# Scatters declared independent, and the gathers of the conditional pairs put into their first product

## The chip, the cores and the metric

The kernel runs on one core of one Trainium2 chip. Its time is the device time of one execution in microseconds (us); less is better. Three runs of the kernel before took 545.45, 544.35 and 548.22 us, a median of 545.45 us.

## What is computed

An attention block reads 32 states per head into 512 tokens and the tokens into the states, with two softmaxes. The rows that it makes, 8 x 544 = 4352 of 512 numbers, go to a mixture of 8 experts. Each row belongs to one expert, which depends on the row itself and, through a gate, on the row before it:

```python
for b in range(B):
    prev_e = -1
    for s in range(S):
        fresh_e = int(np.argmax(logits[b, s]))
        if s == 0 or local_gate[b, s] < 0.5:
            e = fresh_e
        else:
            e = prev_e if prev_e >= 0 else fresh_e
        prev_e = e
        ...
        h = np.maximum(x[b, s] @ w1[e], 0.0)
        out[b, s] = p[e] * (h @ w2[e])
```

`w1[e]` is 512 x 1024 and `w2[e]` is 1024 x 512; everything is in 32-bit floats. `p[e]` is the softmax probability of the expert.

## The kernel before, in words

**Stages.** `Attention` makes the rows and writes them to `rows` in device memory. `Routing` finds each row's expert and gives it a slot: rows of one expert are put together in pairs of 128-row blocks, and what is left over goes in tiles of 32 rows. `slots.tok` holds the number of the row in each slot (for whole rows), `slots.row` the same for quarters of rows. `experts` (from line 770) then works through the pairs and tiles. A row has one slot; a slot without a row has a number beyond the table, which the scatter leaves out.

**Pairs.** A pair is two blocks, b = 0 and 1, of rows of one expert. At least 10 pairs (`NPMIN`) and at most 23 (`NP`) can be needed; the number is known only on the chip. `pair` (L1095) is called for pairs 0 to 8 in a plain loop (L1171), each with a 32-row tile between its halves and with `late=True`. Pair 9 and those after it come from `last` (L1174): pair 9 always, and each further one inside a `tc.If(pairs > u + 1)` (L1178), nested; there `late=False`. In this data 16 pairs run, 0 to 15, so the branch to pair 16 is not taken.

**One pair.** Both products of a pair are done with seven half-size products instead of eight. `strassen` (L987) is the first product, `second_half` (L1030) the second, both through `seven` (L946), which runs the products in the order 1, 5, 6, 2, 7, 3, 4 (with `apart`, 1, 5, 6, 2, 3, 7, 4) and lets ScalarE or VectorE (DVE) take each result from PSUM. The sums of quarter matrices that this needs are DVE's: of w1 in `first_sums` (tiles `a`, in two parts), of w2 in `second_sums` (tiles `c`, at the start of a pair), of the turned rows in `column_sums` (tiles `xs`, from `x_t`). All sums come from the helper `add` (L917), so the profile shows them at L918.

**Preparing the next pair.** While pair u computes, SP loads the weights of pair u + 1 (`load`, L851), DVE makes their sums, and POOL gathers the rows: `quarter` (L807) is one indirect DMA of 128 quarter rows into `xgs_`, which has two buffers, for even and odd pairs. `gathers(v, b)` (L818) is a generator of four of these for block b of pair v. Each waits for a value: `tick` (L823) is a one-element copy on POOL of a result of the products, so a gather is issued behind that result. `seven` hands results to `gets` at four places: behind products 5, 6, 2 and 7; with `apart`, behind 5, 6, 2, 3 and 4, of which a generator uses the first four. In pair u, the first product gathers block 1 of pair u + 1, and the second product block 0 of pair u + 2 (L1134, `gets`).

In the second product, `ready(0)` (L1120) makes the first two sums of the next `a`, turns both gathered blocks into `x_t` (`turned`, L837) and makes the `xs` sums; `ready(1)` makes the last two sums of `a`. Both are for pair u + 1, also when that pair does not come.

**Scatters.** A finished block `ys[b]` goes to its rows of `out` by an indirect DMA on POOL: `scatter` (L982), shown at L984. Block 0 is scattered inside the second product, block 1 behind it: with `late=True` it is handed to the next pair, which issues it in its first product (`waiting`), with the tile's scatter (`Tile.scatter`, L912, shown at L914) after it; with `late=False` it is issued at the end of the pair, before the branch. All scatters write `out`. In the order that is kept between operations on one tensor, each waits until the one before it has been written.

**Order.** The order of each engine's work is that of the program (`tc.manual_schedule`, L85). POOL's queue in a conditional pair u is: the scatter of block 1 of the pair before, four ticks and gathers of the first product, a `drain` (L1140), ticks and gathers of the second product, and between them the scatter of block 0. SP's queue holds the weight loads.

Of the kernel before, what the change touches and what calls it, by code (L numbers as in the profile page):

```python
# [23 lines left out]
NT = B * T  # L24
# [9 lines left out]
Q = P // SQ  # L34
PAIR = 2 * P

NPMIN = NT // PAIR - E * (PAIR - 1) // PAIR

NP = (NT + (E - 1) * (PAIR - 1)) // PAIR
# [132 lines left out]
class Attention:  # L172
# [80 lines left out]
    def get(self, name, *key):  # L253
        return self.of[(name, *key)]
# [515 lines left out]
def experts(ctx, late, tc, bank, w1, w2, rows, slots, route, routing, out):  # L770
    nc = tc.nc
# [28 lines left out]
    def places(u, i):  # L800
# [3 lines left out]
        (w11, w12, w21, w22), sums = [[ring[i][(n + j) % RING] for j in js] for js in (range(4), range(4, 7))]  # L804
        return ((w11, w12), (w21, w22)) if i == 0 else ((w11, w21), (w12, w22)), sums

    def quarter(to, k, i):  # L807

        nc.gpsimd.indirect_dma_start(out=to.rearrange("p x k -> p (x k)"), out_offset=None,  # L809
                                     in_=rows.rearrange("n q x -> (n q) x"),  # L810
                                     in_offset=bass.IndirectOffsetOnAxis(ap=slots.row[:, k, i:i + 1], axis=0))
# [6 lines left out]
    def gathers(u, b):  # L818


        for i in range(Q):
            value = yield
            nc.gpsimd.tensor_copy(tick, value)  # L823
            quarter(xgs_[u % 2][:, b, i], 2 * u + b, i)
        while True:
            yield

    def begun(generator):
        next(generator)
        return generator  # L830


    def turned(u):
        for b in range(2):
            to = x_t[:, :, b * P:b * P + P]
            if u:
                nc.vector.transpose(to.rearrange("p k (i t) -> p k i t", i=Q),  # L837
                                    xgs_[u % 2][:, b].rearrange("p i x k -> p k i x"))
                continue

            for h, copy in enumerate((nc.vector.tensor_copy, nc.scalar.copy)):
                t = bank(P, KT * P // 2)
                for j in range(KT // 2):
                    nc.tensor.transpose(t[:, j * P:j * P + P], first[b][:, 2 * h + j::KT], route.ident)
                copy(to[:, 2 * h:2 * h + 2, :], t.rearrange("p (k t) -> p k t", k=KT // 2))
# [5 lines left out]
    def load(u, i, quarters=slice(4)):  # L851

        e = index(slots.experts[0:1, u - 1:u] if u else slots.again if i else slots.expert)
        q = places(u, i)[0]
        for half, other in [((0, 0), (0, 1), (1, 0), (1, 1)), ((0, 0), (1, 0), (0, 1), (1, 1))][i][quarters]:
            to = q[half][other]
            if i:
                w = w2[bass.ds(e, 1), half, :, other]
            else:
                w = w1[bass.ds(e, 1), half, :, other * KT * F // 4:(other + 1) * KT * F // 4]  # L860
            nc.sync.dma_start(out=to.rearrange("p k f -> p (k f)"), in_=w.rearrange("o p x -> (o p) x"))

    class Tile:
# [6 lines left out]
        def gather(self):  # L870
            quarter(self.x_g, self.k, self.q)
# [39 lines left out]

        def scatter(self, y):  # L912
            at = bass.IndirectOffsetOnAxis(ap=slots.row[:, self.k, self.q:self.q + 1], axis=0)
            nc.gpsimd.indirect_dma_start(out=out.rearrange("n (q x) -> (n q) x", q=Q), out_offset=at, in_=y,  # L914
                                         in_offset=None, bounds_check=NT * Q - 1, oob_is_err=False)

    def add(out, a, b, op=Alu.add):  # L917
        nc.vector.tensor_tensor(out, a, b, op=op)  # L918
# [12 lines left out]
    def first_sums(u, part):  # L931
        ((a11, a12), (a21, a22)), to = places(u, 0)
        if part == 0:
            add(to[0], a21, a22)
            add(to[1], to[0], a11, Alu.subtract)
        else:
            add(a21, a11, a21, Alu.subtract)
            add(to[2], a12, to[1], Alu.subtract)

    def column_sums():  # L940
        sums_of_rows(xq, (xs[0], xs[1], xs[3]), lambda b22, b12: add(xs[2], b22, b12, Alu.subtract))

    def second_sums(u):
        sums_of_rows(*places(u, 1), lambda b22, b12: add(b12, b12, b22, Alu.subtract))
# [36 lines left out]

    def scatter(b, y):  # L982
        to = bass.IndirectOffsetOnAxis(ap=slots.tok[:, b:b + 1], axis=0)
        nc.gpsimd.indirect_dma_start(out=out, out_offset=to, in_=y, in_offset=None, bounds_check=NT - 1,  # L984
                                     oob_is_err=False)

    def strassen(u, others, gets, waiting):  # L987
        ((a11, a12), (a21, a22)), was = places(u, 0)
# [41 lines left out]
    def second_half(u, others, ready, gets, behind, late):  # L1030
# [19 lines left out]
        def second_whole(i, t):  # L1050
            if i == 1:
                others(1)
                scaled(ys[0][:, low], p0)(t)
                ready(0)
                if late:
                    ready(1)
                return ys[0]
            elif i == 4:
                add(ys[1][:, high], r7, r5)
            elif i == 2:  # L1060
                nc.vector.scalar_tensor_tensor(ys[0][:, high], t, p0, r2, Alu.mult, Alu.add)
                scatter(2 * u, ys[0])
                return ys[0]
            else:
                if late:
                    scaled(ys[1][:, low], p1)(t)
                else:
                    nc.vector.scalar_tensor_tensor(ys[1][:, low], t, p1, r7, Alu.mult, Alu.add)
                behind.append(lambda: scatter(2 * u + 1, ys[1]))
                return ys[1]  # L1070
# [6 lines left out]
    def plain(u, gets):  # L1077

        a = places(u, 0)[0]
        for b in range(2):  # L1080
            for n in range(2):
                hps = bank()
                for i in range(4):
                    for j in range(KT):
                        nc.tensor.matmul(hps[:, i * P:i * P + P], lhsT=a[n][j // 2][:, j % 2, i * P:i * P + P],
                                         rhs=x_t[:, j, b * P:b * P + P], start=(j == 0), stop=(j == KT - 1))
                nc.scalar.activation(hqs[2 * b + n].rearrange("p m t -> p (m t)"), hps, Act.Relu)
                for get in gets:
                    get(hqs[2 * b + n][:, 0, :])
        add(hs[0], c12, h22)  # L1090
        add(hs[1], hs[0], h11, Alu.subtract)
        add(c12, c12, h11, Alu.subtract)
        add(hs[2], h21, hs[1], Alu.subtract)

    def pair(u, ahead=True, tile=None, after=None, waiting=(), late=True):  # L1095


        behind = []
        if ahead:
            for i in range(2):  # L1100
                load(u + 1, i, slice(2) if u or i else slice(4))
        second_sums(u)
        if tile:
            tile.turned()

        def between():
            if u == 0:
                next(probabilities)
            if tile:
                tile.one()  # L1110
            if after:
                after.load(0)
                after.gather()

        def others(i):

            if ahead:
                load(u + 1, i, slice(2, 4))

        def ready(i):  # L1120
            if ahead:
                first_sums(u + 1, i)
                if i == 0:
                    turned(u + 1)
                    column_sums()

        def getting(v, b):
            if not ahead or v >= NP:
                return lambda value: None
            generator = begun(gathers(v, b))  # L1130
            return lambda value: generator.send(value[0:1, 0:1])


        gets = [getting(u + 1, 1), getting(u + 2, 0)]  # L1134
        if u:
            strassen(u, others, gets[0], waiting)
        else:
            plain(u, [getting(1, 0), gets[0]])
        if not late:
            nc.gpsimd.drain()  # L1140
        between()
        second_half(u, others, ready, gets[1], behind, late)
        if u == 0:
            next(probabilities)
        if tile:
            behind.append(tile.two())
        if after:
            after.load(1)
        if not late:
            for results in behind:  # L1150
                results()
        return behind
# [18 lines left out]
    for u in range(NPMIN - 1):  # L1171
        waiting = pair(u, True, tiles[u], tiles[u + 1] if u + 1 < NTILE else None, waiting)

    def last(u, waiting=()):  # L1174

        pair(u, u + 1 < NP, waiting=waiting, late=False)
        if u + 1 < NP:
            with tc.If(pairs > u + 1):  # L1178
                last(u + 1)
# [35 lines left out]
```

## Time and profile before

| | |
|---|---|
| median of three runs | 545.45 us (544.35 to 548.22) |
| the profiled execution | 547.97 us, of which its span (first to last instruction) 546.2 us |
| granted TensorE clock, mean | 0.996 |
| busy: PE, PEld, DVE, ACT, POOL | 525.4, 459.2, 382.4, 173.7, 318.4 us |
| gathers of quarter rows for pairs (`xg`, L809) | 132, 1197 ns each in the mean |
| scatters of blocks (L984) | 32, 1097 ns each in the mean |
| scatters of tiles (L914) | 9 |

The engines are PE (TensorE's products), PEld (its weight loads), DVE (VectorE), ACT (ScalarE), POOL (GpSimd) and SP (SyncE, which issues the weight loads). In the timeline a line gives the start in us, the duration, the engine, the line of the program, the operation, what it writes and reads, how many, and in brackets the idle time of that engine before it and what ended it. The busy time of a DMA on POOL is the time for which POOL works at issuing it; the landing comes later. In the busy time by stretch, the columns are the stretch, its length, the busy time of PE, PEld, DVE, ACT and POOL (with the number of instructions), the clock, the busy share of the DMA engines and GB/s. A releaser in brackets is inferred; where the engine named had long been done, it was something else, often a DMA.

### The profile page before, as it was taken

The page shows a single profiled execution, that of the slowest core. Times are in us where ns is not written, and L with a number is a line of the kernel's source. Part 1 is how long each engine was busy: PE and PEld are TensorE (multiplying, and loading weights), DVE is VectorE, ACT ScalarE, POOL GpSimd, SP SyncE. Part 2 cuts the span into 40 slices and gives each one's busy share as a digit, 9 for nine tenths or more (in the row PEclk, how much of TensorE's full clock was granted, in tenths as well). Part 3 has the DMA queues.
Part 4 walks back from the last instruction along what each step waited for, and adds up shares of the span by engine and source line. Part 5 has one row for each costly group of instructions (what it writes and reads, how often), then busy time and mean ns, then how long its engine had stood idle before and what let it go on. Part 6 is the DMA issues. An engine that isn't in the chain of part 4 may idle for free. (4 is left out here: it accounts for less than half of the span.)

```text
span 546.2 us, 12964 instructions
## 1 busy us (share of the span) xinstructions
PE 525.4 (96%) x4921; PEld 459.2 (84%) x4921; DVE 382.4 (70%) x622; ACT 173.7 (32%) x357; POOL 318.4 (58%) x386
## 2 busy tenths in 40 slices
PE   7789889999999999999999999999999999999993
PEld 2567666988989898989898989889999998999992
DVE  6999876757666657575665848486767767787773
ACT  6788654112223222222222222313232222223220
POOL 7788602564684756565665656576564645545454
PEclk9999999999999999999999999999999999999998
DMA  8999777699989899897979797974748484666743
GB/s 315 411 341 350 260 254 237 235 395 393 403 285 377 309 340 361 293 387 267 388 276 389 269 385 281 354 235 166 232 168 283 146 286 153 243 201 223 233 158 104
DMA packets 49002, 155.46 MB, mean 285 GB/s; under 512 B 6865, under 2 KB 8017, under 8 KB 45602
## 3 DMA queue, kind: packets, MB, share of 16 engines
q1 hardware_dynamic: 41234, 135.78, 68.0%
q0 software_dynamic: 7552, 18.69, 9.7%
q8 instruction: 41, 0.67, 0.5%
q14 instruction: 31, 0.25, 0.1%
q10 hardware_dynamic: 144, 0.07, 0.1%
HBM read 136.68 MB, written 17.89 MB: 283 GB/s over the span
## 5 line engine op out<-in xcount | busy, mean ns | idle before, releaser
L809 POOL DMA_INDIRECT xg<-rows,row x132 | 158.0, 1197 | 26.5 <-issue 25.6
L918 DVE TENSOR_TENSOR a<-a,a 128x1024 f32<-128x1024 f32 x64 | 77.1, 1225 | 29.7 <-DMA a<-in_w_dram 28.3
L1001 PE MATMUL ps<-xt,a 128*128 128x128 f32 x720 | 88.8, 276 | 0.0
L1001 PE MATMUL sum<-xs,a 128*128 128x128 f32 x720 | 87.7, 275 | 0.0
L1001 PEld LDWEIGHTS ps<-xt,a 128*128 128x128 f32 x720 | 84.5, 192 | 1.9 <-issue 1.4
L1001 PEld LDWEIGHTS sum<-xs,a 128*128 128x128 f32 x720 | 84.0, 192 | 0.0
L918 DVE TENSOR_TENSOR c<-c,c 128x1024 f32<-128x1024 f32 x64 | 75.4, 1220 | 3.6 <-issue 2.9
L1041 PE MATMUL ps<-c,h 128*128 128x256 f32 x312 | 74.7, 382 | 0.0
L1041 PEld LDWEIGHTS ps<-c,h 128*128 128x128 f32 x312 | 58.0, 190 | 10.9 <-issue 3.7
L984 POOL DMA_INDIRECT out_dram<-y,tok x32 | 35.1, 1097 | 48.5 <-DVE c L918 34.0
L1041 PE MATMUL ps<-c,hs 128*128 128x256 f32 x256 | 60.5, 379 | 0.0
L1041 PEld LDWEIGHTS ps<-c,hs 128*128 128x128 f32 x256 | 48.6, 190 | 6.6
L1041 PE MATMUL sum<-c,h 128*128 128x256 f32 x200 | 47.2, 379 | 0.0
L1041 PEld LDWEIGHTS sum<-c,h 128*128 128x128 f32 x200 | 38.0, 190 | 5.2
L918 DVE TENSOR_TENSOR h<-s,s 128x512 f32<-128x512 f32 x15 | 10.5, 698 | 44.8 <-ACT s L1024 37.6
L823 POOL COPY tick<-r 1x1 f32<-1x1 f32 x41 | 20.7, 504 | 32.9 <-ACT r L1046 30.7
L823 POOL COPY tick<-s 1x1 f32<-1x1 f32 x45 | 18.5, 410 | 35.6 <-ACT s L1024 35.5
L952 ACT COPY sum<-ps 128x256 f32<-128x256 f32 (+1 forms) x31 | 14.3, 461 | 70.2 <-PE ps L1001 52.2
L837 DVE STREAM_TRANSPOSE xt<-xg 128x512 f32<-128x512 f32 x32 | 34.0, 1088 | 2.5 <-DMA xg<-rows,row 2.4
L432 PE MATMUL p<-sd,a 128*128 128x256 f32 x128 | 32.1, 390 | 0.0
L1046 ACT ACTIVATE r<-sum,prob 128x256 f32<-128x256 f32 x32 | 15.2, 474 | 52.0 <-PE sum L1041 29.7
L1041 PE MATMUL sum<-c,hs 128*128 128x256 f32 x128 | 30.2, 379 | 0.0
(230 smaller groups left out, 755.2 us busy)
## 6 DMA issues: line engine op xcount, KB each, us to landing
a<-in_w_dram SPq DMA_DIRECT2D x68, 512.0 KB
c<-in_w_dram SPq DMA_DIRECT2D x68, 512.0 KB
at<-in_w_dram SPq DMA_DIRECT2D x18, 1024.0 KB
ct<-in_w_dram SPq DMA_DIRECT2D x18, 1024.0 KB
x_t<-in_xt_dram SPq DMA_DIRECT2D x16, 512.0 KB
x_n<-in_xn_dram SPq DMA_DIRECT2D x8, 1024.0 KB
rows<-xr SPq DMA_DIRECT2D x32, 256.0 KB
xg<-rows,row POOLq DMA_INDIRECT x132
```

What stands on the lines that cost most here:

```text
L432: self.nc.tensor.matmul(v[:, d], lhsT=self.get("a", b, u)[:, c * P:c * P + P], rhs=self.sd[:, b, d], start=True, stop=True)
L809: nc.gpsimd.indirect_dma_start(out=to.rearrange("p x k -> p (x k)"), out_offset=None, in_=rows.rearrange("n q x -> (n q) x"), in_offset=ba ...
L823: nc.gpsimd.tensor_copy(tick, value)
L837: nc.vector.transpose(to.rearrange("p k (i t) -> p k i t", i=Q), xgs_[u % 2][:, b].rearrange("p i x k -> p k i x"))
L918: nc.vector.tensor_tensor(out, a, b, op=op)
L952: nc.scalar.copy(y, x)
L984: nc.gpsimd.indirect_dma_start(out=out, out_offset=to, in_=y, in_offset=None, bounds_check=NT - 1, oob_is_err=False)
L1001: nc.tensor.matmul(to[:, m * P:m * P + P], lhsT=w[:, j, m * P:m * P + P], rhs=x[:, j, :], start=begin and m == 0 and j == 0, stop=(m == FK ...
L1041: nc.tensor.matmul(to, lhsT=x[:, m, :], rhs=w[:, m, :], start=begin and m == 0, stop=(m == FK // 2 - 1), skip_group_check=True)
L1046: nc.scalar.activation(to, t, Act.Copy, scale=p)
```

## The change

Two things are changed. Every scatter, of blocks and of tiles, is put in one group, and declared to have no dependence on the others in it. And in pairs with `late=False` the gathers are placed anew: the second product gathers nothing (`getting(NP, 0)` gives a function that does nothing), and from pair 10 on the first product gathers both blocks of pair u + 1, one quarter of block 0 and one of block 1 at each of the four places. Pair 9 still gathers block 1 of pair 10 in its first product, since pair 8 has gathered block 0. Pairs 0 to 8 gather as before.

```diff
+    def apart(scatter):
+
+        tc.declare_no_dep(scatter.ins, group="scatters", reason="a token has one slot, so scatters write other rows")
+        tc.add_to_no_dep_group("scatters", scatter.ins)
+
...
         def scatter(self, y):
             at = bass.IndirectOffsetOnAxis(ap=slots.row[:, self.k, self.q:self.q + 1], axis=0)
-            nc.gpsimd.indirect_dma_start(out=out.rearrange("n (q x) -> (n q) x", q=Q), out_offset=at, in_=y,
-                                         in_offset=None, bounds_check=NT * Q - 1, oob_is_err=False)
+            apart(nc.gpsimd.indirect_dma_start(out=out.rearrange("n (q x) -> (n q) x", q=Q), out_offset=at, in_=y,
+                                               in_offset=None, bounds_check=NT * Q - 1, oob_is_err=False))
...
     def scatter(b, y):
         to = bass.IndirectOffsetOnAxis(ap=slots.tok[:, b:b + 1], axis=0)
-        nc.gpsimd.indirect_dma_start(out=out, out_offset=to, in_=y, in_offset=None, bounds_check=NT - 1,
-                                     oob_is_err=False)
+        apart(nc.gpsimd.indirect_dma_start(out=out, out_offset=to, in_=y, in_offset=None, bounds_check=NT - 1,
+                                           oob_is_err=False))
...
         gets = [getting(u + 1, 1), getting(u + 2, 0)]
+        if not late:
+            if u > NPMIN - 1:
+                both = getting(u + 1, 0), gets[0]
+                gets[0] = lambda value: [get(value) for get in both]
+            gets[1] = getting(NP, 0)
         if u:
             strassen(u, others, gets[0], waiting)
```

## The prediction, made before the result was known

> **What bounds the kernel now.** I read the page first, then the busy time by stretch, then the waits of each engine, then the timelines of POOL and DVE over the last pair. The page shows TensorE busy almost throughout:
>
> ```profile
> PE 525.4 (96%) x4921; PEld 459.2 (84%) x4921; DVE 382.4 (70%) x622; ACT 173.7 (32%) x357; POOL 318.4 (58%) x386
> ```
>
> The busy time by stretch puts the rest at the end. A conditional pair (16 pairs run, 0 to 15; 9 to 15 go through `last`) has no PE idle; the last 11.2 us have almost only idle:
>
> ```profile
> 510.00:535.00 25.00, 25.00 (x172) 23.50 (x171) 18.32 (x23) 6.41 (x12) 13.47 (x21) 1.00 0.63 215
> 535.00:546.20 11.20, 2.27 (x11) 1.66 (x9) 3.23 (x4) 0.47 (x1) 4.27 (x5) 0.78 0.24 75
> ```
>
> The waits of PE between 120 and 546 us name none at all. One conditional pair follows another every 24.59 us (first weight load of the first product at 487.71 and 512.30). So a cover taken from any other engine is free, until it reaches PE; what can be won lies behind PE's last product, in the tail. POOL, from the scatter of pair 14's first block to the last scatter:
>
> ```profile
> 511.75 1.07 POOL L984 DMA_INDIRECT out_dram<-y,tok  x1 [0.30 <-issue]
> ...
> 519.98 1.10 POOL L984 DMA_INDIRECT out_dram<-y,tok  x1 [5.86 <-DVE c L918]
> 521.06 0.18 POOL L823 COPY tick<-s 1x1 f32<-1x1 f32 x1
> ...
> 524.53 1.34 POOL L809 DMA_INDIRECT xg<-rows,row  x1 [0.16 <-issue]
> ...
> 526.56 1.25 POOL L809 DMA_INDIRECT xg<-rows,row  x1 [0.16 <-issue]
> ...
> 536.14 1.27 POOL L984 DMA_INDIRECT out_dram<-y,tok  x1 [0.30 <-issue]
> ...
> 541.01 1.02 POOL L984 DMA_INDIRECT out_dram<-y,tok  x1 [2.30 <-DMA out_dram<-y,tok]
> ```
>
> The second scatter of a pair waits for the first one's write: 5.86 us at 519.98, 2.30 us at 541.01. The first is put down to DVE, but the line L984 by itself shows POOL's sequencer in a semaphore wait from 510.4 for 8.78 us, to 519.2, while the row's data was ready at 513.2. Everything behind it on POOL (ticks, gathers) waits too. DVE over the same time:
>
> ```profile
> 515.45 4.74 DVE L918 TENSOR_TENSOR c<-c,c 128x1024 f32<-128x1024 f32 x4
> ...
> 524.34 0.69 DVE L1015 SCALAR_TENSOR_TENSOR hs<-h,h 128x512 f32<-128x512 f32 x1
> ...
> 526.27 0.68 DVE L918 TENSOR_TENSOR hs<-h,hs 128x512 f32<-128x512 f32 x1
> 526.88 2.54 DVE L918 TENSOR_TENSOR a<-a,a 128x1024 f32<-128x1024 f32 x2
> ...
> 530.99 1.10 DVE L837 STREAM_TRANSPOSE xt<-xg 128x512 f32<-128x512 f32 x1 [0.56 <-DMA xg<-rows,row]
> ...
> 537.31 0.48 DVE L1068 SCALAR_TENSOR_TENSOR y<-ps,prob,r 128x256 f32<-128x256 f32 x1 [0.80 <-issue]
> 537.71 2.40 DVE L918 TENSOR_TENSOR a<-a,a 128x1024 f32<-128x1024 f32 x2
> ```
>
> See three ends together. The gather begun at 524.53 ends at 525.87, 0.84 after DVE's sum that ran when it began (525.03). That of 526.56 ends at 527.81, 0.86 after the sum ended (526.95). The scatter of 519.98 ends at 521.08, 0.89 after the last c sum (520.19). Begun while DVE has no such sum, a gather takes 0.97. I read: a POOL transfer that begins inside a sum of two SBUF tiles gets on only when that sum ends, and then needs 0.87. A tick likewise (525.88 for 0.52, to 526.40; that sum ended at 526.36), else 0.18.
>
> **The change, part by part.** *Scatters in pairs 0 to 8.* POOL's wait before the tile scatters goes (23.8 us over 6 at L914). PE waits for nothing there, and the next ticks wait for ScalarE's results: 0, covered by PE.
>
> *The scatter held in pairs 9 to 14.* 34.0 us over 6 leave POOL, none from PE directly; they make room for the gathers.
>
> *Gathers moved.* In pairs 10 and on, the four quarter gathers of the first block move from the preceding pair's second product into the first product, so 8 instead of 4 follow the four results there; pair 9 keeps 4, and the second products have none. In sum 52 instead of 56 from pair 9 on: 4 x (0.18 + 0.16 + 0.97 + 0.16) = 5.9 us of POOL, off the path. DMA: 4 x 64 KB move into a stretch whose engines are busy 0.63, at 215 GB/s 1.2 us; SP's weight loads share them, and no wait of DVE on a weight stands in the list after 385. I cost that at 0; PE's and DVE's spare hides it.
>
> When do the 8 gathers land? Pair 15's clock, first tick after ScalarE's copy at 516.93 (L1024, 516.34 + 0.59). With DVE as now: two ticks and gathers stretch over the c sums (ends at 517.82, 519.01, 520.19) to 521.4, the next five end at 522.7, 524.2, 525.9, 527.8, and, past the two a sums, 530.3, the eighth at 531.6. Now the last ends at 527.81 and DVE sees it 3.18 later; so blocks arrive at 533.5 and 534.8, not before 529.33 and at 530.99. DVE stands still meanwhile, and its later work (four xs sums 1.6, L1061, L1068, a and c sums) slips. In the next pair the c sums end some 1.1 later, then settle 2.4 later (522.6), and the chain is: gathers end at 520.0, 522.3, 524.2, 525.9, 527.8, 530.3, 531.6, 532.9. The first block lands at 534.7, the second at 536.05. The nearest rows for landing after a gather's end are 2.07 (381.45 to 383.52) and 3.35 (429.34 to 432.69), so 535.0 to 536.3.
>
> Does PE wait? Its next first product begins at 512.52 + 24.59 = 537.1; that product uses the first block alone (ready 534.7 + 1.1 = 535.9), the next product, 1.8 later, needs the first xs sum (537.7 against 538.9). Spare 1.2 us; 0. Were the wait in the program for both blocks, 537.2 against 537.1. Next late after that would be the weight sums: the last a sum 542.5 against the fifth product at 544.3.
>
> *Tail.* In pair 15 the last scatter no longer waits for the other's landing (540.18). If the gathers came in time: row ready 537.79, + 0.3 = 538.1 instead of 541.01: -2.9. But they are for a pair that does not come, and DVE works through them first. With the second block at 536.05, xs ends at 538.8, L1061 at 539.3, L1068 at 540.1; the first scatter ends at 540.6, the second begins at 540.9, inside an a sum that ends at 541.3, and ends at 542.2, against 542.03 now: +0.2. At a landing 1.0 earlier, 541.1: -0.9. The ends are -2.9 and +0.2; between, I take the middle of the two landings, -0.4. The branch and the closing steps behind the last scatter (5.19 us from its begin to the span's end) stay.
>
> Sum: 547.97 us of the profiled execution (span 546.2 + 1.8) - 0.4 = 547.6. That execution lies 2.5 above the median, so I set it on the median: 545.45 - 0.4 = 545.0.
>
> **The notes against the trace.** The row is the gathers' end 0.87 behind DVE's sum. The Trainium skill, "GPSIMD Engine Reference", section "Key points", says that GpSimd shares its SBUF interfaces with VectorE and contends with instructions of two SBUF inputs; it speaks against moving POOL's work beneath the c sums, and the trace agrees. Without that rule the tail would give -2.9, with it -0.4. For the scatter's landing the row says 4.04 us (536.14 to 540.18). The skill, "DMA: Bandwidth & Descriptors", section "Anatomy of one DMA", fits 2.0 us + bytes / 436e3; for 256 KB that is an estimate of 2.6, by which the wait removed at the end would be 0.95 long. The measured 4.04 decides.
>
> **The rivals.** (1) *Gathers in time, tail in full.* For it: POOL starts 4.1 us earlier than now (516.95 against 521.06). Against: the stretching above. 545.45 - 2.9 = 542.6, up to 544.
>
> (2) *Slower: the eight gathers reach PE.* Place: the transposes of x_t before the next first product, in the 4 to 5 passages 10-11 to 14-15. It decides from 1.2 us more than I reckon (0 if both blocks are waited for): one more sum boundary (1.19) on the chain, or landing 4.4 after the end. One us past the point costs 1 x 5, with +0.5 in the tail: 545.45 + 5.5 = 551; at 0.5 us, 548.5; at 1.7, 554.5. For it: chains of four took 8.8 us at 181.6 to 190.4, 2.2 each; 8 x 2.2 = 17.6 from 516.95 ends at 534.5, 1.6 above my 532.9. Against: DVE, standing still for the blocks, runs no sums at the chain's end.
>
> (3) *The declaration takes no wait away across the branches.* Then the chain begins at 521.06 as now, ends at 534.2 or, with slipped sums, 535.7; the blocks land up to 538.9, PE waits 1.8 to 3 us x 5, the last scatter is 4 to 5 later: 558 to 566. Against: the wait is between two writes of `out` alone, which is what is declared.
>
> (4) A gain above 1% would need more than the 2.9 of the tail; nothing in the trace offers it, other than the spread of the runs (544.35 to 548.22).
>
> **How the numbers follow.** My forecast 0.46, at 543.5 to 546; rival 1 0.18; rival 2 0.26, half of it above 550.9; rival 3 0.06; rival 4 0.04. About 1% (5.5 us) is what a measurement of this kernel can tell from no change: faster 0.04, within 0.46 + 0.18 + 0.13 = 0.77, slower 0.13 + 0.06 = 0.19. The range goes from the full tail, 542.5, to 552, where rival 2 has some 0.10 above it; with rivals 3 and 4, 0.20 is left out.
>
> **What would show it.** Right: no wait before the scatter near 513 to 516; eight gathers between 517 and 533 in pair 15, ends behind DVE's sums; DVE waiting for xg 3 to 5 us before L837; PE's pairs still 24.59 apart; the last scatter begun at 539.8 to 541. Wrong: pairs over 25 us with PE waiting for DVE at L1001 (rival 2); a semaphore wait still before L984 (rival 3); DVE's transposes near 531 and the last scatter at 538 (rival 1).

## The result, and the profile after

The changed kernel takes 549.6 us in the median of 22 runs (543.66 to 562.95), the kernel before 546.5 (543.89 to 548.22) in 22 runs on the same chips. The ratio is 1.0045, with a 95% interval of 1.0029 to 1.0061: some 2.5 us slower, where the forecast was 0.4 us faster. Seven of the 22 executions lie at 559 to 563 us and stand outside this ratio; a trace of such an execution is shown further down. The profiled execution took 549.85 us with a span of 548.1, against 547.97 and 546.2 before.

Busy time of the engines and the stretches of the changed kernel (columns: PE, PEld, DVE, ACT, POOL busy, granted clock, DMA share, GB/s):

```profile
PE 527.2 (96%) x4921; PEld 461.0 (84%) x4921; DVE 382.3 (70%) x622; ACT 173.9 (32%) x357; POOL 314.2 (57%) x378
```

```profile
510.00:535.00 25.00, 25.00 (x171) 23.51 (x170) 17.70 (x23) 6.42 (x12) 17.72 (x18) 1.00 0.61 210
535.00:548.10 13.10, 1.93 (x9) 1.34 (x8) 6.01 (x10) 0.47 (x1) 4.09 (x2) 0.71 0.13 47
```

PE still has no idle time up to 536.9, and its waits between 120 and 548 us name none. The time from PE's end to the span's end has grown from 8.9 us (537.27 to 546.2) to 11.1 (536.93 to 548.1). Behind 535 us VectorE (DVE) now does 6.0 us of work, 3.2 before: the work that slipped behind the later gathers. From the waits from 385 us on:

```profile
POOL out_dram L989 <- DVE y L923: 22.5, 4, 6.0
DVE xt L842 <- DMA xg<-rows,row: 21.0, 10, 4.2
...
POOL out_dram L989 <- DVE y L1073: 15.8, 3, 7.0
```

Lines stand 5 to 10 further down than before (L989 is the block scatter, L842 the transposes, L1066 and L1073 the last two scalings of y). No scatter waits for another scatter's landing any more; DVE waits for the moved gathers instead, up to 4.2 us, without PE seeing it. Pair 15 begins 0.34 us earlier than before (512.17); the other +2.2 us are the tail. VectorE and POOL in it:

```profile
535.86 1.10 DVE L842 STREAM_TRANSPOSE xt<-xg 128x512 f32<-128x512 f32 x1 [1.64 <-DMA xg<-rows,row]
...
538.47 0.48 DVE L1066 SCALAR_TENSOR_TENSOR y<-ps,prob,r 128x256 f32<-128x256 f32 x1
538.86 0.42 DVE L923 TENSOR_TENSOR y<-r,r 128x256 f32<-128x256 f32 x1
539.19 0.48 DVE L1073 SCALAR_TENSOR_TENSOR y<-ps,prob,r 128x256 f32<-128x256 f32 x1
539.59 2.35 DVE L923 TENSOR_TENSOR a<-a,a 128x1024 f32<-128x1024 f32 x2
539.76 3.08 POOL L989 DMA_INDIRECT out_dram<-y,tok  x1 [7.00 <-DVE y L1073]
543.15 1.00 POOL L989 DMA_INDIRECT out_dram<-y,tok  x1 [0.30 <-issue]
```

The first scatter's row is ready at 538.95 (L1066), and POOL's sequencer ends its semaphore wait for it at 538.99, yet the scatter begins at 539.76. The profile puts this wait down to L1073, but in pair 13, shown further down, the scatter begins 0.37 us before L1073 does; it waits for L1066. At 539.76 the two a sums already run, which are for a pair that does not come, and the scatter ends at 542.84, 0.90 us after the second of them. Only then comes the second scatter, 2.14 us later than before the change (541.01).

### The profile page after: what moved, and what is told of

Read it like the earlier page. It is cut to its first block, busy times and chain, and to the rows that moved or that the text cites. A ratio compares the mean times of both kernels' runs of the same rounds, so it can differ in the third digit from the quotient of the medians.

```text
span 548.1 us, 12909 instructions
## 1 busy us (share of the span) xinstructions
PE 527.2 (96%) x4921; PEld 461.0 (84%) x4921; DVE 382.3 (70%) x622; ACT 173.9 (32%) x357; POOL 314.2 (57%) x378
## 5 line engine op out<-in xcount | busy, mean ns | idle before, releaser
L814 POOL DMA_INDIRECT xg<-rows,row x128 | 154.6, 1208 | 27.6 <-issue 27.6
L989 POOL DMA_INDIRECT out_dram<-y,tok x32 | 40.0, 1250 | 61.1 <-DVE y L923 22.5
L842 DVE STREAM_TRANSPOSE xt<-xg 128x512 f32<-128x512 f32 x32 | 34.1, 1092 | 21.8 <-DMA xg<-rows,row 21.8
L828 POOL COPY tick<-s 1x1 f32<-1x1 f32 x63 | 20.9, 332 | 46.9 <-ACT s L1029 46.8
L828 POOL COPY tick<-r 1x1 f32<-1x1 f32 x27 | 13.4, 496 | 41.8 <-ACT r L1051 41.6
```

Source lines behind the costliest of these rows:

```text
L989: apart(nc.gpsimd.indirect_dma_start(out=out, out_offset=to, in_=y, in_offset=None, bounds_check=NT - 1, oob_is_err=False))
```

## The experiments

Theory A: the loss is the tail, made by the moved gathers. Theory B: the loss is in the independence of the scatters itself, wherever their wait is gone. Every kernel was timed beside the kernel before on the same chip; kernels timed together there are called a session. "Tail" is the time from pair 15's first product to the span's end, in the profiled execution: 33.7 us before, 35.9 after.

**The two halves of the change.** The first kernel is the changed one without the block of five lines that moves the gathers; the second has the gathers moved and

```
-            apart(nc.gpsimd.indirect_dma_start(...))
+            nc.gpsimd.indirect_dma_start(...)
```

in both scatters.

> Only the scatters are declared independent; the gathers stay where they were before the change. Theory A (the loss is in the tail: the moved gathers of the pair that never comes make DVE's last row late, and the scatters then begin beneath the weight sums of that same pair): the last scatter begins near 539.0 instead of 541.01, ends 0.9 after the last a sum, near 541.0 instead of 542.03; ratio to before 0.997 to 0.999. Theory B (the loss is in the independence itself: scatters close together, or the tile scatters of pairs 0 to 8 issued earlier, cost what the wait saved): ratio 1.003 to 1.006 as with the whole change. Pairs stay 24.59 us apart under both.

> Only the gathers are moved; the scatters wait for each other as before. Theory A: the scatter of block 1 waits for the landing of the first, some 7.4 us after it, until about 521 of pair 15's clock, so the eight gathers end near 536, 3 us later than with the whole change; the blocks come after PE's next first product should begin (537.1), PE waits for x_t, pairs are 26 to 28 us apart from pair 11 on, and the last scatter is 4 to 5 us later: ratio 1.02 to 1.036. Theory B: without the independence nothing is lost, ratio 0.998 to 1.002.

Measured: the declaration alone 1.019 (1.0143 to 1.0237), which neither theory had; its tail is 31.3 us, 2.4 shorter than before, as A has it, but its pairs 1 to 8 took 29.4 to 31.0 us each instead of 28.73. The gathers alone: 1.072 (1.0674 to 1.0767), pairs 1 to 8 at 28.7 to 29.5 us and pairs 11 to 14 at 29.8 to 35.0. PE's wait in it, from 385 us on:

```profile
PE ps L1006 <- DVE xt L842: 21.8, 4, 7.4
```

So the moved gathers need the independence: with the scatters' old wait the chain of eight gathers begins 8.5 to 17.2 us into a pair instead of 4.6, and PE waits for the transposes. And with the scatters' old wait pairs 1 to 8 are not late, in the session in which the declaration alone makes them so.

**The tail: the sums beside the last scatters, and the gathers of the pair that does not come.** In the first kernel the two a sums of the next pair move out of the pair ahead, to the head of the conditional pair:

```
-        if not late:
-            ready(1)
...
+        if u > NPMIN - 1:
+            first_sums(u, 1)
```

The second has no gathers in pair 15 (it leaves out those for a pair 16, which these inputs do not use):

```
-            if not ahead or v >= NP:
+            if not ahead or v >= (NP if late else 16):
```

> The whole change, and the last two a sums of the next pair are issued at the start of that pair, inside its branch, so that the last pair does not run them. Theory A: the two last scatters no longer lie beneath a sums; the first takes 1.0 instead of 3.08 us, the second begins at 541.1 instead of 543.15, the span is 2.0 us shorter than with the whole change, ratio to before 0.999 to 1.001. Theory B: no change from the whole change, 1.003 to 1.006. A third, that gathers and not sums hold POOL at the end: the first scatter still takes 3 us.

> The whole change without the gathers for pair 16 and later, which this data never uses; DVE turns what the buffer held instead. Theory A: DVE is not held in the last pair, its last row is ready at 537.8 as before the change, the last scatter begins at 538.6 beneath the a sums and ends between 539.9 and 541.0 instead of 544.15; ratio to before 0.994 to 0.998. Theory B: the last scatter gains at most the 0.7 us that the late row costs, ratio 1.002 to 1.005.

Measured: 1.0218 (1.0156 to 1.028) and 1.0158 (1.0113 to 1.0203), both with late pairs 1 to 8 (28.7 to 31.3 and 29.1 to 30.9 us) like the declaration alone beside them, so the ratios say nothing of the tail. The traces do. With the sums gone the last two scatters are:

```profile
551.16 1.02 POOL L989 DMA_INDIRECT out_dram<-y,tok  x1 [7.17 <-DVE y L1073]
552.49 1.00 POOL L989 DMA_INDIRECT out_dram<-y,tok  x1 [0.30 <-issue]
```

1.02 us instead of 3.08, and a tail of 34.3: 1.6 us of the 2.2 come back, and it is still 0.6 longer than before the change. Without the last gathers the tail is 31.5, near that of the declaration alone. Theory A's account of the tail stands; what made pairs 1 to 8 late was open.

**Controls, and the independence in the conditional pairs alone.** The next session had the changed kernel itself, and three variants: independence only in pairs 9 to 15, with the moved gathers and without them,

```
+        if alone:
+            apart(it)
...
-                scatter(2 * u, ys[0])
+                scatter(2 * u, ys[0], not late)
```

and the whole change with the tile's scatter issued in the second half:

```
-              gets, apart=not late)
+              gets, waiting, apart=not late)
...
-            strassen(u, others, gets[0], waiting)
+            strassen(u, others, gets[0], waiting[:1])
...
-        second_half(u, others, ready, gets[1], behind, late)
+        second_half(u, others, ready, gets[1], behind, late, waiting[1:])
```

> The changed kernel as it is, as a control on the chip of the runs beside it. Theory A (the whole loss is the tail: the two last scatters stand behind the longer gather chain): pairs 0 to 8 stay at 28.7 us each, ratio 1.003 to 1.006. Theory B (the scatters' independence in pairs 0 to 8, where their wait went away, makes TensorE's results late wherever those scatters fall beside loads and gathers, as in the three kernels whose pairs took 30.5 to 31): here too pairs of 28.7 in one execution and of 30.5 in another, ratio between 1.005 and 1.025.

> Scatters independent only in the conditional pairs 9 to 15; in pairs 0 to 8 the block scatters and the tile scatters wait for each other as before; gathers moved as in the change. Theory A: no different from the changed kernel, 1.003 to 1.006, pairs 0 to 8 as there. Theory B: pairs 0 to 8 at 28.7 to 29.1 us in every execution, none near 559 us, ratio 1.003 to 1.006, by the tail alone.

> The change whole, but the tile's scatter is issued behind the sixth product of the second half, some 8 us later in a pair, and waits for nothing. Theory A: 1.003 to 1.006 whatever is done in pairs 0 to 8. Theory B with the early tile scatter as the cause (it began at 12.4 us of a pair, before the change at about 16.3): pairs at 28.7 to 29.1, 1.003 to 1.006. Theory B with another cause (the block scatters, or the gathers that no longer stand behind the wait): pairs of 30.5 to 31 remain, ratio 1.015 to 1.025.

> Scatters independent in the conditional pairs alone, gathers where they were before the change. Theory A and Theory B agree on the tail: without the moved gathers the last two scatters follow TensorE's end at once (6.5 us from the last product's issue to the end, in the kernel with the declaration alone, against 8.9 before), 2.4 us less than before: ratio 0.994 to 0.998. Under Theory B pairs 0 to 8 are at 28.7 to 29.1; Theory A has nothing against that. A ratio above 1.003 would say that the independence costs also in the conditional pairs.

Measured: 1.0039 (1.0014 to 1.0064), 1.0026 (0.9994 to 1.0057), no ratio for the third (five of its six executions at 559 to 562 us), 0.9952 (0.9936 to 0.9968) for the fourth. All four have pairs 1 to 8 of 28.73: here the independence in pairs 0 to 8 neither cost nor gained, and Theory B was not seen. But the second kernel too had four of nine executions at 559 to 562 us, so these do not come from the independence in pairs 0 to 8. The fourth kernel is the fastest of them, 0.5% below the kernel before: its tail is 31.4 us, and its last two scatters (the trace's lines stand two further down) need no more than

```profile
533.99 1.02 POOL L989 DMA_INDIRECT out_dram<-y,tok  x1 [0.30 <-DVE y L1068]
...
537.35 1.75 POOL L989 DMA_INDIRECT out_dram<-y,tok  x1 [1.02 <-DVE y L1075]
```

**The halves and the tail once more.** The declaration alone and the sums in the branch as above, and the fourth kernel with the sums in the branch.

> The declaration alone once more (all scatters independent, gathers as before the change), because the first time its pairs 0 to 8 took 30.5 us on a chip on which the changed kernel itself was not run. If independence in pairs 0 to 8 costs 1.8 us a pair wherever it is run: ratio 1.015 to 1.024, pairs at 30.5 to 31. If that belongs to that chip: pairs at 28.7, the tail 2.4 us shorter than before, ratio 0.994 to 0.998.

> The whole change, with the two sums of weights that a conditional pair's product needs taken out of the pair ahead and put at the head of the pair itself, so that none runs beside the last two scatters. Theory A (the loss is the first scatter of the last pair held under these sums, 3.08 us, and the second behind it): scatters of 1.0 us each, the second ends 2.4 us after the last y instead of 4.5, the end 1.8 to 2.1 us earlier than the changed kernel, ratio 0.999 to 1.003. Rival (the loss is the chain of gathers, transposes and sums itself, and the scatters' length is hidden by it): ratio stays at 1.003 to 1.006. With pairs 0 to 8 at 30.5 us again, about 1.020 and nothing is told by the ratio, only by the tail.

> Scatters independent in the conditional pairs alone, gathers where they were before the change, and the two sums at the head of the conditional pair. In the kernel without the last of these the last scatter took 1.75 us and ended under the sums; 0.7 us less here: ratio 0.992 to 0.996 against 0.9952 measured. If the sums at the head of a pair make the first products wait for them, pairs 10 to 15 grow beyond 24.59 us and the ratio is above 1.

Measured: 0.9984 (0.9965 to 1.0002), 1.001 (0.9979 to 1.0041), 0.9968 (0.9954 to 0.9981). The very kernel that took 559.3 us in the first session took 545.0 here, on the same chip, with pairs of 28.73: the lateness of pairs 1 to 8 comes with the session. With the sums away from the last scatters the whole change is at 1.001, where A has it, but its interval reaches into the rival's 1.003 to 1.006, and six of its eleven executions, which stand outside the ratio, were at 557.6 to 561.8; that the two last scatters take 1.02 and 1.00 us is in the trace again. The last kernel's last scatter took 1.02 instead of 1.75 us; against the 0.9952 of the other session no gain can be told.

**The sums ahead of the transposes**, where VectorE stands still for the gathers:

```
-        if not late:
-            ready(1)
...
                 first_sums(u + 1, i)
                 if i == 0:
+                    if not late:
+                        first_sums(u + 1, 1)
                     turned(u + 1)
```

> The whole change, with the two sums of weights that stand behind a conditional pair's last y on VectorE put ahead of its transposes, where VectorE stands still for the moved gathers (up to 4.2 us). Theory A (what decides is whether a scatter begins beside VectorE's sums): in the last pair no sum follows the last y, so both last scatters take 1.0 us, and the end comes at least 1.8 us earlier than in the changed kernel: ratio 0.997 to 1.002. In the pairs before it the four c sums now follow the last y at once, so a late y still puts a scatter beneath sums, 3 to 4 us long, and executions in which each chain of gathers begins later than the one before (TensorE waiting for the transposes in the last pairs, 557 to 562 us) remain. Rival (the two a sums alone are what holds the scatters, and what lets the chains slip): scatters of 1.0 to 2.0 us in all conditional pairs, chains beginning 4.55 us into each pair, no execution above 552 us, ratio 0.995 to 0.999. Second rival (the sums now delay the transposes): transposes end beyond 23 us of a pair already in pair 10, ratio above 1.01.

Measured: 1.0472 (1.0432 to 1.0511), pairs 1 to 8 at 29.9 to 31.2 us and pairs 10 to 14 at 26.4 to 26.9. The next session had it beside the changed kernel and the kernel with independence in the conditional pairs alone, gathers in place.

> The whole change with the two sums of weights ahead of the transposes, once more, beside the changed kernel itself. If the lateness of pairs 0 to 8 belongs to chip and call: pairs 0 to 8 at 28.7 us as in the changed kernel beside it. Then, if what decides is whether a scatter begins beside VectorE's sums: last two scatters 1.0 us each, chains of gathers beginning 4.55 us into every conditional pair (in the last run they did), no pair over 24.7: ratio 0.995 to 1.000. If the sums delay the transposes by themselves (in the last run they ended at 24.2 us of a pair, the sums having begun late): pairs over 26 us and ratio above 1.01 here too.

> The changed kernel as it is, the control. Pairs 0 to 8 at 28.7 and ratio 1.003 to 1.006 if this call is like those in which it was measured; pairs of 30.5 and 1.02 or more if it is like the calls in which the declaration alone took 559 us.

> Scatters independent in the conditional pairs alone, gathers as before the change, once more: 0.993 to 0.998 if the gain of 0.5% measured once is the tail's 2.4 us. In pairs 0 to 8 its scatters wait for each other as before, so here they should stay at 28.7 to 29.1 us even if the control beside it shows 30.5.

Measured: 1.0464 (1.0427 to 1.0501), 1.0258 (1.0215 to 1.0302), 0.9966 (0.9937 to 0.9995). With the sums ahead the last two scatters take 1.02 and 1.00 us and all chains begin at 4.55 us, but pairs 10 to 14 are at 26.7 to 26.9. The forecast's second alternative has that number, but not the cause: PE does not wait for the transposes there, but for a copy on ScalarE:

```profile
PE sum L1046 <- ACT sum L957: 10.4, 6, 1.8
```

ScalarE's work ahead of that copy (L1024) begins 4.48 us after the modelled end of the product that it reads (504.50 against 500.02); in the changed kernel's execution at the start it was 0.04 (475.69 against 475.65). Why, no row says.

Here the changed kernel itself has pairs 1 to 8 at 28.7 to 31.4 us, and the kernel beside it, whose scatters still wait for each other there, 28.7 to 29.5. So in such sessions Theory B holds as well: the independence in pairs 0 to 8 costs 13 us (eight periods, 245.2 against 231.9 us, one execution of each). One pair of each, first the changed kernel (pair begun at 193.4):

```profile
204.19 1.95 PE L1006 MATMUL sum<-xs,a 128*128 128x128 f32 x16
204.49 0.97 POOL L814 DMA_INDIRECT xg<-rows,row  x1 [0.16 <-issue]
205.77 1.02 POOL L919 DMA_INDIRECT out_dram<-yt,row  x1 [0.30 <-issue]
...
206.07 1.48 PE L897 MATMUL ps<-at,xtt 128*32 128x256 f32 x18
...
207.75 0.61 PE L897 MATMUL ps<-at,xtt 128*32 128x256 f32 x3 [0.20 <-issue]
...
209.16 1.07 PE L897 MATMUL ps<-at,xtt 128*32 128x256 f32 x11 [0.81 <-issue]
...
209.28 0.60 ACT L1024 ACTIVATE h<-sum 128x512 f32<-128x512 f32 x1 [4.63 <-remote]
```

then the one with dependent scatters in these pairs (begun at 190.0, lines two further down):

```profile
200.81 1.95 PE L1008 MATMUL sum<-xs,a 128*128 128x128 f32 x16
201.08 0.97 POOL L814 DMA_INDIRECT xg<-rows,row  x1 [0.16 <-issue]
...
202.69 1.93 PE L897 MATMUL ps<-at,xtt 128*32 128x256 f32 x32
...
203.13 0.60 ACT L1026 ACTIVATE h<-sum 128x512 f32<-128x512 f32 x1 [1.84 <-PE sum L1008]
...
206.62 1.02 POOL L919 DMA_INDIRECT out_dram<-yt,row  x1 [4.57 <-DVE hs L923]
```

The two are alike up to the tile's scatter, which begins at 12.4 us of the pair, just before the tile product, or at 16.6, behind it. With the early scatter the tile product (L897) takes 4.2 instead of 1.9 us, and the result of the product before it, which by the profile ended at 206.14, reaches ScalarE at 209.28, 3.1 us later (0.4 in the other kernel). No wait of PE names a cause. The kernel with the tile scatter later, beside one more control, was to tell whether that scatter is it:

> The change whole, the tile's scatter issued behind the sixth product of the second half, as in the run before of this edit, whose pairs were at 28.7 us like those of the changed kernel beside it, and told nothing of pairs 0 to 8. If the control's pairs 0 to 8 are late here (30.5 to 31.4 us): at 28.7 to 29.3 in this kernel if the tile scatter's moment is the cause, ratio 1.003 to 1.02 by the conditional pairs alone; at 30.5 or more, ratio above 1.02, if the cause is something else in the independence, such as any transfer on POOL at 12.4 us (the gather for the next tile then stands there). If the control's pairs are at 28.7, nothing is told.

> The changed kernel as it is, the control: pairs 0 to 8 at 28.7 us and 1.003 to 1.006, or at 30.5 to 31.4 and 1.02 to 1.03 as in the last call.

Measured: 1.0023 (0.9992 to 1.0054), and a control with pairs 0 to 8 at 28.73, so that nothing was told of them. But the control's median is 558.66 us, five of six executions at 558.5 to 560.4, and its profiled execution (560.28 us) is one of those. Its granted clock is 0.985, against 0.984 in the execution shown at the start, and the kernel before, timed beside it, stayed between 544.5 and 551.7 us: nothing speaks for a slower chip. PE's wait in it names what the prediction had as its second rival:

```profile
PE ps L1006 <- DVE xt L842: 7.5, 2, 5.3
```

Here are the first scatters of pairs 10 to 14 in it, from POOL's timeline:

```profile
412.38 1.02 POOL L989 DMA_INDIRECT out_dram<-y,tok  x1 [5.33 <-DVE y L923]
...
438.33 4.22 POOL L989 DMA_INDIRECT out_dram<-y,tok  x1 [6.68 <-DVE y L1073]
...
464.95 4.22 POOL L989 DMA_INDIRECT out_dram<-y,tok  x1 [7.41 <-DVE y L1073]
...
493.53 4.22 POOL L989 DMA_INDIRECT out_dram<-y,tok  x1 [9.76 <-DVE y L1073]
...
523.43 4.22 POOL L989 DMA_INDIRECT out_dram<-y,tok  x1 [10.26 <-DVE y L1073]
```

Beside the execution shown at the start, all in us into the pair, from the timelines of POOL and DVE:

| pair | 548.1 span: transposes end | its first scatter took | next pair's first tick | 558.5 span: transposes end | its first scatter took | next pair's first tick |
|---|---|---|---|---|---|---|
| 10 | 21.6 | 1.02 | 4.55 | 21.5 | 1.02 | 4.55 |
| 11 | 22.2 | 1.02 | 4.55 | 22.8 | 4.22 | 6.56 |
| 12 | 21.7 | 1.03 | 4.55 | 24.9 | 4.22 | 8.57 |
| 13 | 21.6 | 1.03 | 4.55 | 28.9 | 4.22 | 11.34 |
| 14 | 23.1 | 4.22 | 6.79 | 31.9 | 4.22 | 10.29 |

The rows show one mechanism in both. If the moved gathers land in time, VectorE must wait for PE's last product before L1073; the first scatter begins in that gap and takes 1.0 us. If the transposes end some 0.5 us later (at 22.8 us of the pair or after; 22.3 was still in time), VectorE runs from y straight into the a sums, the scatter begins under them and takes 4.22 us, the next pair's gathers queue behind it, 2.0 to 2.8 us later than the chain before, land later too, and so on: each pair hands its delay on, until PE waits. In the first execution the slip comes in pair 14, so that only pair 15 inherits it: that is the +2.2 us. In the second it comes in pair 11, and PE waits in pairs 14 and 15. Three variants, in sessions with pairs 1 to 8 on time, had a profiled execution of 557.6 to 562.0 us (the sums in the branch once more, and twice the tile's scatter later); they slip from pair 11 too. VectorE and POOL where the first execution is in time (pair 13) and where it is not (pair 14):

```profile
486.12 0.48 DVE L1066 SCALAR_TENSOR_TENSOR y<-ps,prob,r 128x256 f32<-128x256 f32 x1
...
487.41 1.03 POOL L989 DMA_INDIRECT out_dram<-y,tok  x1 [5.47 <-DVE y L923]
...
487.78 0.48 DVE L1073 SCALAR_TENSOR_TENSOR y<-ps,prob,r 128x256 f32<-128x256 f32 x1 [0.79 <-PE ps L1046]
488.18 2.35 DVE L923 TENSOR_TENSOR a<-a,a 128x1024 f32<-128x1024 f32 x2
...
512.15 0.48 DVE L1066 SCALAR_TENSOR_TENSOR y<-ps,prob,r 128x256 f32<-128x256 f32 x1
...
512.88 0.48 DVE L1073 SCALAR_TENSOR_TENSOR y<-ps,prob,r 128x256 f32<-128x256 f32 x1
513.27 2.35 DVE L923 TENSOR_TENSOR a<-a,a 128x1024 f32<-128x1024 f32 x2
513.44 4.22 POOL L989 DMA_INDIRECT out_dram<-y,tok  x1 [6.91 <-DVE y L1073]
```

In both the scatter begins 0.81 us after L1066's end; the a sums begin 1.58 us after that end in the one and 0.64 in the other.

The changed kernel also shows what it does when no chain slips: in the session with late pairs 0 to 8 (the execution of 560.02 us) every first scatter of pairs 10 to 15 took 1.02 to 1.03 us and every chain began at 4.55 us. Its tail is 32.1 us, 1.5 shorter than before the change, 3.8 shorter than in the execution shown at the start:

```profile
549.69 0.48 DVE L1066 SCALAR_TENSOR_TENSOR y<-ps,prob,r 128x256 f32<-128x256 f32 x1
...
550.98 1.02 POOL L989 DMA_INDIRECT out_dram<-y,tok  x1 [5.66 <-DVE y L923]
551.31 2.35 DVE L923 TENSOR_TENSOR a<-a,a 128x1024 f32<-128x1024 f32 x2
552.30 1.10 POOL L989 DMA_INDIRECT out_dram<-y,tok  x1 [0.30 <-POOLq L1188]
```

So the moved gathers by themselves do not lengthen the tail; the slip does.

## Why the prediction was wrong

**Failed: the tail (-0.4 predicted, +2.2 measured).** The step that failed is "the first scatter ends at 540.6, the second begins at 540.9, inside an a sum". It took some 0.3 us from the row's release to the scatter's begin; measured 0.81. The 0.3 is what a scatter showed that stood directly behind a gather (536.14 before the change). With the gathers moved away POOL's sequencer stands in a wait for the row, and the scatter begins 0.77 us behind that wait. The trace of before has this size wherever the sequencer waited so, in the prediction's own rows too: the wait ended at 519.2 and the scatter began at 519.98, the landing was at 540.18 and the scatter began at 541.01. So the first scatter, not the second, fell under the a sums, by 0.17 us. And it did not get on behind the first sum, which by the prediction's reading of the three ends would give an end at 541.7, but behind both, at 542.84: 3.08 us instead of 1.02. The second scatter stood behind it, 543.15 instead of 540.9. The runs with the sums elsewhere agree: both last scatters 1.0 us, a tail of 34.3 instead of 35.9.

**Luck: the walk up to it.** The last gather was to end at 532.9 and ended at 532.76, xs at 538.8 (538.55), L1061, now L1066, at 539.3 (538.95). But two errors cancelled in that. The forecast's chain, 20.4 us into the pair at its end, was 1.4 us too long: in pairs 10 to 14 the last gather ended at 18.95. And the chain of pair 15 began 2.2 us late, at 6.79 instead of 4.55, behind pair 14's scatter of 4.22 us, of which the forecast knew nothing. With neither the slip nor the long scatter the tail was 1.5 us shorter than before, in the one profiled execution that shows it.

**Half right: gathers moved, PE's spare 0.** In the executions inside the ratio, pairs 10 to 14 stay at 24.59 us, as worked out. The step that failed in the others is the spare, which is not a reserve of 1.2 us to be used once: a delay of about 0.5 us in one chain comes back as 2 us in the next, through the scatter ahead of its gathers. The second rival had its place and its sign right, and its price (548.5 to 554.5) too small for the executions in which it came, 558.5 to 563 us: it added one us per passage where the delay grows from passage to passage.

**Right only in some sessions: scatters in pairs 0 to 8, "0, covered by PE".** Where the ratio of 1.0045 was measured it held: pairs of 28.73, against 28.73 to 29.09 in the profile before. In three sessions, in which the kernel before took 548.8 to 549.9 us instead of 546.1 to 547.2, pairs with independent scatters mostly took 30.5 to 31.5 us; kernels with dependent scatters there, run in two of the three, had 28.7 to 29.5. PE itself was the cover, and there PE's own results came late; no row of the profile before priced that.

**Right: the waits removed (34.0 us of POOL), and the third rival excluded.** No scatter waits for a landing any more. What that is worth by itself shows where the gathers stay: a tail 2.1 to 2.4 us shorter, ratios of 0.9952, 0.9966 and 0.9984 in three sessions (the last with an interval that reaches 1.0002). The prediction's -2.9 for the full tail was near; it went to the moved gathers, which won nothing that PE could see.

**Open.** What differs between sessions in which pairs 0 to 8 are late and those in which they are not. The late pairs, and the 26.8 us pairs with the sums ahead of the transposes in the same sessions, have in common that POOL's transfers follow each other without a pause beside full weight loads; that this is the cause was only argued. It cannot be the whole of it: in such a session pairs 10 to 14 of the changed kernel stayed at 24.59 us, with POOL busy for 15.4 us of a pair and a DMA share of 0.64, against 13.2 us and 0.55 in the late pairs with the sums ahead. Whether the tile's scatter alone brings it was tried, but in sessions that did not show the lateness. Why the transposes end at 22.3 us of a pair behind one chain and at 22.8 behind another was not settled either. The traces narrow it down: in pairs 13 and 14 of the execution at the start the gathers end at the same moments of the pair (the seventh at 17.64 us), but VectorE's first transpose, which waits for them to land, begins at 19.38 us in the one and at 20.98 in the other. So it is the landing and not POOL's queue that differs.

## What to carry to other kernels

Removing a false wait between scatters pays where the queue's end is the kernel's end; declare it there (conditional pairs, gathers left in place: 0.9952 and 0.9966) and be careful with a wait that lies under a busy engine: removing it in pairs 0 to 8 gained nothing in some sessions and cost 13 us in another. When work is moved ahead on a queue, ask what its lateness hands on to the next round: a chain that queues behind its own predecessor's results has no spare, only a threshold. And price a queue's instruction by what its neighbours run at the moment it begins, down to tenths of a microsecond, and look whether the change takes away the neighbour behind which its start was hidden.

## What the runs showed of the hardware

A scatter for which POOL's sequencer stood in a semaphore wait of its own (a row EVENT_SEMAPHORE at the scatter's line) began 0.74 to 0.78 us after the end of that wait in all but one of 157 cases, 15 of them in the trace of before; where the trace has no such row, 0.28 us after the last write of its data (82 cases). Counted are scatters before which POOL stood idle for more than 0.45 us. How long it stood idle does not decide: the long form came after 1.45 us (of a wait of 2.0 us), the short one after 4.7.

An indirect transfer that begins beneath VectorE's sums of two SBUF tiles need not get on when the running sum ends. Begun 0.17 us after the a sums began, it passed the end of one sum (3.08 us, in four kernels) or of two (4.22) and ended 0.9 us behind the next one; but begun 0.16 us after c sums, with the sums ahead of the transposes, it took 1.95 us and ended behind the first, and begun 0.36 us after a sums 1.75 us, also behind the first. What decides how many it passes was not settled. The Trainium skill, "GPSIMD Engine Reference", section "Key points", says that GpSimd shares its SBUF interfaces with VectorE and contends with instructions of two SBUF inputs. The runs agree, and show that in a dense row of such sums one transfer can be held for three of them.

A result of PE reached ScalarE 3.1 us after its last matmul's modelled end (209.28 against 206.14), at a granted clock of 1.00 and with no engine named for the wait; in the kernel with the sums ahead of the transposes it was 4.48 us (504.50 against 500.02).
